# Starting every SBUF tile that TensorE reads at a multiple of 256 bytes, in a gated mix of sliding attention and a GEGLU FFN

## The chip, the cores and the metric

The kernel runs on one core of one Trainium2 chip. The metric is the device time in microseconds of one execution, as the median of several runs. Profiles are of one execution each, whose own time stands beside its span (from the first to the last instruction).

## The reference

For one sequence of 2,048 tokens with 512 channels in float32:

```python
g = sigmoid((x * gate_w).sum(-1))
qkv = x @ wqkv                       # 32 heads of 16 channels
# each query sees 8 keys: itself and 2, 4, ... 14 tokens back (those that exist)
a = softmax(q . k / 4, masked) . v @ wo
b = (gelu(x @ w_gate) * (x @ w_up)) @ w_down     # 1,792 hidden channels
out = g * a + (1 - g) * b
```

## The kernel before

**Split numbers.** Each float32 operand of a matmul is split into a rounded half `hi` and a rest `lo`, both of TensorE's faster float32 kind. A product is three matmuls: hi by hi, hi by lo, lo by hi. `split` (line 78) does that: ScalarE copies (line 82), VectorE subtracts (line 83).

**Halves of the tokens.** The work runs twice, for even tokens (`par` 0) and odd ones (`par` 1). Each half is a projection of x to keys and queries, values, and again keys and queries (`project`, three blocks `cb` 0, 1, 2), and then the FFN in 14 steps `f` of 128 hidden channels (`ffn`, `gate_up`, `down`). Between the two halves stand the second half's projections and the output projection of the first (`finish`, line 638).

**The matmuls.** `qkv_mm` (line 179) has 128 tokens of x as weights and 512 columns of `wqkv` as the moving operand; for `cb` 1, the values, two calls of 258 and 256 columns (line 205; the 257th column of the first is the gate's logit). `product` (line 411) has 128x128 of the gate and up weights as weights and 512 tokens of x, or of sums of x, as the moving operand; seven such products make an FFN step, by a scheme that saves the eighth. `down` (line 450) has hidden channels by tokens as weights and a row of `w_down` as the moving operand.

**The tiles.** Buffers come from one pool; `tl(tag)` (line 53) takes the next buffer of a tag, with the sizes of `COLS` and the counts of `BUFS` (lines 48 to 51). Tiles stand one behind the other in SBUF in the order in which their tags are first used. What TensorE reads:

- `A` (x, hi and lo), `S` (sums of x, also half of the weights of `cb` 0), `rt` (x of two chunks);
- `g0` and `g1`, two buffers each: gate and up weights of an FFN step, hi beside lo. Between FFN halves they hold split chunks of `wqkv` (`rooms`, line 137), each 2 x 258 = 516 columns wide;
- `d`: `w_down` of a step, and the weights of `cb` 2; `hh` and `hl`, six each: hidden channels, or attention's output; at `cb` 1 also the fourth chunk of the values' weights; `c`: split `wo` (and scratch).

**What sets the order.** In the first FFN half, weights come from HBM to `raw` (lines 349, 350, GpSimd's queue), VectorE combines quarters of them (360), ScalarE writes their negative as `lo` (380), a DMA on GpSimd's queue adds `raw` to it (381, an accumulate), ScalarE writes `hi` (383). The split tiles are stored to HBM (`keep`, line 392, SP's queue) and loaded back in the second half (line 376). Attention (lines 241 to 298) runs on VectorE in pieces that `pull` (327) hands out between the matmuls; keys, queries and values go through HBM (lines 194 and 196 on ScalarE's queue, 229 to 234 on SP's). A scheduler orders the recorded instructions of each engine, with attention at low priority.

Of the kernel before, what the change touches and what calls it, by code (L numbers as in the profile page):

```python
# [9 lines left out]
F32 = mybir.dt.float32  # L10
# [5 lines left out]
P = 128  # L16
S, D, F = 2048, 512, 1792
H, DH, W = 32, 16, 8
NT = S // P
NP = NT // 2  # L20
KC = D // P
FC = F // P
CU = 16 * DH
WQ = CU + 2
WT = KC * WQ
UC = 128
UH = UC // DH
NU = D // UC
WARM = 31
# [7 lines left out]
QW = 2 * P  # L37
# [3 lines left out]
def tile_gated_mix(ctx: ExitStack, tc: tile.TileContext, xt, wqkv, wff, wo, out):  # L41
    nc = tc.nc
    ctx.enter_context(nc.allow_non_contiguous_dma(reason="rows of 512 bytes"))
    pool = ctx.enter_context(tc.tile_pool(name="sb", bufs=1))
# [2 lines left out]

    BUFS = {"A": 6, "S": 8, "g0": 2, "g1": 2, "d": 4, "raw": 2, "hh": 6, "hl": 6, "c": 4, "s": 3,
            "r": 2, "rt": 4, "p": 4, "lg": 2}
    COLS = {"A": 1024, "S": 1024, "g0": 6 * WQ, "g1": 8 * WQ, "c": 2 * WQ, "d": 1024, "raw": 8 * QW,  # L50
            "hh": 2 * WQ, "hl": 2 * WQ}

    def tl(tag, dt=F32):
        return pool.tile([P, COLS.get(tag, 512)], dt, name=tag, bufs=BUFS[tag])

    def pair(tag):
        t = tl(tag, F32R)
        return t[:, :512], t[:, 512:1024]

    def bank(tag):  # L60
        return psum.tile([P, 512], F32, name=tag, bufs=BUFS.get(tag, 1))


    warm = pool.tile([P, P], mybir.dt.bfloat16, name="warm")
    nc.vector.memset(warm, 0.0)
    idle = bank("p")
    for _ in range(WARM):
        nc.tensor.matmul(idle[:, :P], warm, warm, start=True, stop=True)
    zero = pool.tile([W, UC], F32, name="zero")
    nc.vector.memset(zero, 0.0)  # L70
# [7 lines left out]
    def split(eng, hi, lo, raw, copy=None):  # L78
        if copy:
            copy(hi, raw)  # L80
        else:
            nc.scalar.activation(hi, raw, AF.Copy)
        eng.tensor_tensor(lo, raw, hi.bitcast(F32), op=OP.subtract)
# [3 lines left out]
    for par in range(2):  # L87
        for hh in range(2):
            for n, t in (("k", KS), ("v", VS)):
                t[par, hh] = dram.tile([2, W + S // 2, UC], F32, name=f"{n}s{par}{hh}")  # L90
                for c in range(2):
                    nc.gpsimd.dma_start(t[par, hh][c, :W], zero)
            QS[par, hh] = dram.tile([2, S // 2, UC], F32, name=f"qs{par}{hh}")
        for u in range(NU):
# [42 lines left out]
    def rooms():  # L137

        def of(*tags):
            for tag, n in tags:  # L140
                t = tl(tag, F32R)
                yield from (t[:, i * 2 * WQ:(i + 1) * 2 * WQ] for i in range(n))
        cols = of(("g1", 4))
        for _ in range(2):
            yield next(cols), next(cols)
        for _ in range(2):
            yield pair("S")
        cols = of(("g0", 3), ("g0", 3), ("hh", 1), ("hl", 1))
        for _ in range(KC):
            yield next(cols), next(cols)  # L150
        for _ in range(KC):
            yield pair("d")

    def load_cb(cb, kc, tag, room, dma=nc.sync):
        hi, lo = WC[cb, kc] = next(room)
        raw = tl(tag)
        n = 512
        if cb == 1:
            n = 2 * WQ
            for hh in range(2):  # L160
                dma.dma_start(raw[:, hh * WQ:(hh + 1) * WQ], wqkv[hh, 2, :, kc * WQ:(kc + 1) * WQ])
        else:
            dma.dma_start(raw[:, :n], wqkv[cb // 2, kc // 2, :, kc % 2 * 512:kc % 2 * 512 + 512])
        return lambda: split(nc.vector, hi[:, :n], lo[:, :n], raw[:, :n])
# [8 lines left out]
    def qkv_mm(ps, par, jj, cb, kcs, c0=0, cn=512):  # L173
        t = slice((jj % BT) * P, (jj % BT + 1) * P)
        for kc in kcs:
            xh, xl = X[par, jj // BT, kc]
            wh, wl = WC[cb, kc]
            for n, (a, w) in enumerate(((xh, wh), (xl, wh), (xh, wl))):
                nc.tensor.matmul(ps[:, :cn], a[:, t], w[:, c0:c0 + cn], start=(kc == 0 and n == 0),  # L179
                                 stop=(kc == KC - 1 and n == 2))  # L180
# [4 lines left out]
    def take(ps, par, jj, hh, vals, eng=None):  # L185
        st = tl(next(stages))
        n = CU if vals else 512
        if eng:
            eng.tensor_copy(st[:, :n], ps[:, :n])
        else:  # L190
            nc.scalar.activation(st[:, :n], ps[:, :n], AF.Copy)  # L191
        two = st.rearrange("p (a c d) -> p a c d", a=2, c=2)
        dst = VS[par, hh] if vals else KS[par, hh]
        nc.scalar.dma_start(rows(dst[:, W:], jj), two[:, 0])
        if not vals:
            nc.scalar.dma_start(rows(QS[par, hh], jj), two[:, 1])
        elif not hh:
            nc.scalar.activation(z[:, par, jj:jj + 1], ps[:, CU:CU + 1], AF.Copy)

    def project(par, cb, bg=iter(())):  # L200
        for jj in range(NP):
            if cb == 1:
                for hh in range(2):
                    ps = bank(next(names))
                    qkv_mm(ps, par, jj, 1, range(KC), hh * WQ, (WQ, CU)[hh])
                    take(ps, par, jj, hh, True)
            else:
                ps = bank(next(names))
                qkv_mm(ps, par, jj, cb, range(KC))
                take(ps, par, jj, cb // 2, False)  # L210
            next(bg, None)
            pull(2.7)
        done.add((par, cb))
        if cb == 1:
            en = pool.tile([P, NP], F32, name="en")
            nc.scalar.activation(en, z[:, par], AF.Exp, scale=-1.0)
            nc.vector.tensor_scalar_add(en, en, 1.0)
            nc.vector.reciprocal(g[:, par], en)
            nc.vector.tensor_scalar(gc[:, par], g[:, par], -1.0, 1.0, op0=OP.mult, op1=OP.add)
# [4 lines left out]
    def load_kq(par, u):  # L224
        hh, c = divmod(u, 2)
        k = pool.tile([P, 2 * NP - 1, UC], F32, name="k")
        q = pool.tile([P, NP, UC], F32, name="q")
# [99 lines left out]
    def pull(budget, key=None):  # L327
        credit[0] += budget
        while credit[0] > 0 and (key is None or key not in done):
            with tc.high_priority(offset=-BEHIND):  # L330
                c = next(fill, None)
            if c is None:
                credit[0] = 0.0
                return
            credit[0] -= c
        if key:
            credit[0] = 0.0
# [189 lines left out]
    def before():  # L527

        fetch_x(1, 1)
        yield  # L530
        room_x(1)
        for kc in range(KC):
            load_cb(0, kc, "r", room, nc.gpsimd)()
            yield
# [123 lines left out]


    room = rooms()  # L660
    room_x(0)
    for kc in range(KC):
        first = ((0, P), (P, 512 - P)) if not kc else ((0, 512),)
        sp = load_cb(0, kc, "c", room)
        if not kc:
            XR.update((i, tl("raw")) for i in range(2))
        for blk in range(2):
            for a, n in first if not blk else ((0, 512),):
                o = (2 * blk + kc // 2) * 512 + a
                nc.sync.dma_start(XR[kc % 2][:, o:o + n], xt[blk, :, kc, a:a + n])  # L670
            split_x(0, blk, kc, first if not blk else ((0, 512),), nc.vector.tensor_copy if not (kc or blk) else None)
            if not blk:
                sp()
    ps = [bank(next(names)) for _ in range(NP)]
# [6 lines left out]
    for kc in range(KC):  # L681
        load_cb(1, kc, "c", room)()
# [4 lines left out]
    for kc in range(KC):  # L687
        load_cb(2, kc, "c", room)()
    project(0, 1)
    combine(0)  # L690
    for _ in operands(0, 0):
        pass
    combine(1)
    project(0, 2)
    fetch_d(0)
    room = rooms()
    ffn(0)
    for kc in range(KC):
        load_cb(1, kc, "c", room)()
    project(1, 0, sums_x())  # L700
    fetch_o()
    for kc in range(KC):
# [53 lines left out]
```

## Time and profile before

| | us |
|---|---|
| median of 3 runs | 663.26 (662.86 to 665.01) |
| the profiled execution | 665.45 |
| its span | 663.6 |
| TensorE busy | 623.3 |
| VectorE busy | 518.5 |
| ScalarE busy | 338.8 |
| GpSimd busy | 136.1 |
| mean granted TensorE clock | 0.984 |

In profile lines PE is TensorE, PEld its weight loads, DVE VectorE, ACT ScalarE, POOL GpSimd, SP SyncE; a q behind a name is that engine's DMA queue. A line as `L411` is a line of the kernel. Busy time of TensorE counts overlapping matmuls by modelled ends, so "busy" is not "at its peak"; how far apart neighbouring matmuls start is the better measure of its pace.

### The profile page before, as it was taken

The numbers are of one execution on the slowest core, as the hardware profiler recorded it, in microseconds if no ns is written. First come the engines' busy times: TensorE is split into PE (matmuls) and PEld (weight loads), VectorE is DVE, ScalarE is ACT, GpSimd is POOL, SyncE is SP. The second block draws the span as 40 slices with busy tenths as digits, with TensorE's granted clock in tenths as the row PEclk, the third lists the DMA queues.
The fourth block names the chain that finished last, engine by engine and source line by source line (L and its number), as shares of the span: only waits on it lengthen the run. The fifth ranks groups of instructions, "written<-read, shape, count | busy, mean of one in ns | idle before, by whom it ended". The sixth has DMA issues, their size and how long they took to land.

```text
span 663.6 us, 8115 instructions
## 1 busy us (share of the span) xinstructions
PE 623.3 (94%) x2839; PEld 507.0 (76%) x2839; DVE 518.5 (78%) x567; ACT 338.8 (51%) x581; POOL 136.1 (21%) x161
## 2 busy tenths in 40 slices
PE   8999569998999998988999999799999999999997
PEld 7898447777778786776889888588878888878885
DVE  6939179988799789697984798988998999981241
ACT  5535057574667856558655422234445435444561
POOL 5012013132223222121110001342212222021100
PEclk9999979999999999998999999799999999999999
DMA  8688969999999999995669997954757472543113
GB/s 257 184 248 219 361 191 234 334 315 286 329 303 314 269 365 251 323 268 200 191 199 318 309 330 208 218 179 165 269 190 269 149 258 112 179 142 124 38 58 126
DMA packets 75336, 153.97 MB, mean 232 GB/s; under 512 B 7712, under 2 KB 43168, under 8 KB 71712
## 3 DMA queue, kind: packets, MB, share of 16 engines
q1 hardware_dynamic: 36000, 103.84, 43.9%
q0 software_dynamic: 13184, 37.04, 23.5%
q10 hardware_dynamic: 26112, 12.59, 6.5%
q8 instruction: 22, 0.36, 0.2%
q14 instruction: 18, 0.15, 0.1%
HBM read 80.76 MB, written 56.16 MB: 206 GB/s over the span
## 4 chain that ended last, share of the span: by engine, by line
PE 49%; DMA 26%; DVE 9%; issue 8%; ACT 5%; POOL 2%; ACTq 1%; SPq 0%; POOLq 0%; DVEq 0%
PE p L411 18%; DMA g<-raw 10%; PE p L179 7%; PE acc L179 7%; PE p L450 6%; PE acc L450 5%; PE p L638 3%; PE acc L638 3%; DMA raw<-wff 2%; DMA vs<-s 2%; DMA qs<-s 2%; DMA q<-qs 2%; DMA raw<-xt 2%; DVE prod L281 2%; DMA ws<-g 1%
## 5 line engine op out<-in xcount | busy, mean ns | idle before, releaser
L411 PE MATMUL p<-S,g 128*128 128x512 f32 x672 | 174.1, 400 | 18.9 <-ACT r L191 12.0
L411 PEld LDWEIGHTS p<-S,g 128*128 128x128 f32 x672 | 127.6, 191 | 51.6 <-ACT r L191 12.5
L411 PE MATMUL p<-A,g 128*128 128x512 f32 x504 | 133.4, 399 | 10.2 <-DMA g<-raw 6.2
L411 PEld LDWEIGHTS p<-A,g 128*128 128x128 f32 x504 | 95.0, 190 | 36.4 <-DMA g<-raw 9.4
L246 DVE TENSOR_TENSOR prod<-k,q 128x2048 f32<-128x2048 f32 x32 | 73.0, 2280 | 9.2 <-DMA q<-qs 9.0
L427 POOL TENSOR_TENSOR hl<-c,hh 128x512 fp32r<-128x512 f32 x28 | 45.4, 1622 | 160.4 <-ACT hh L426 117.1
L281 DVE TENSOR_TENSOR prod<-v,lg 128x2048 f32<-128x2048 f32 x32 | 75.0, 2343 | 0.8 <-DMA v<-vs 0.2
L450 PE MATMUL p<-d,hh 128*128 128x512 f32 x224 | 70.0, 401 | 4.9 <-ACT p L444 4.9
L248 DVE TENSOR_REDUCE lg<-prod 128x128 f32<-128x2048 f32 x32 | 73.0, 2281 | 0.3
L450 PE MATMUL acc<-d,hh 128*128 128x512 f32 x224 | 59.1, 395 | 0.0
L450 PEld LDWEIGHTS p<-d,hh 128*128 128x128 f32 x224 | 42.5, 191 | 16.3 <-ACT p L444 6.7
L426 ACT ACTIVATE hh<-c 128x512 fp32r<-128x512 f32 x56 | 35.2, 628 | 34.5 <-DVE c L424 34.1
L424 DVE TENSOR_TENSOR c<-c 128x512 f32<-128x512 f32 x56 | 38.4, 685 | 14.7 <-ACT c L523 14.1
L450 PEld LDWEIGHTS acc<-d,hh 128*128 128x128 f32 x224 | 42.0, 188 | 9.9 <-ACT hh L426 0.3
L463 ACT ACTIVATE rt<-p 128x512 f32<-128x512 f32 x48 | 28.0, 592 | 42.2 <-PE p L450 42.1
L420 DVE TENSOR_TENSOR c<-p,s 128x512 f32<-128x512 f32 x56 | 38.1, 682 | 13.5 <-PE p L411 13.1
L415 ACT ACTIVATE s<-p 128x512 f32<-128x512 f32 x56 | 32.8, 592 | 26.2 <-PE p L411 19.1
L450 PE MATMUL p<-d,hl 128*128 128x512 f32 x112 | 43.3, 401 | 0.0
L285 DVE TENSOR_TENSOR prod<-prod 128x1024 f32<-128x1024 f32 x32 | 39.5, 1235 | 0.3
L381 POOL DMA_DIRECT2D g<-raw x28 | 26.9, 1009 | 37.4 <-ACT g L380 32.3
L360 DVE TENSOR_TENSOR raw<-raw 128x256 f32<-128x256 f32 (+1 forms) x42 | 21.2, 507 | 16.9 <-DMA raw<-wff 11.6
L380 ACT ACTIVATE g<-raw 128x1024 fp32r<-128x1024 f32 (+1 forms) x28 | 26.6, 950 | 15.3 <-DVE raw L360 12.7
(150 smaller groups left out, 975.1 us busy)
## 6 DMA issues: line engine op xcount, KB each, us to landing
ws<-g SPq DMA_DIRECT2D x14, 1024.0 KB, 7.8
g<-ws SPq DMA_DIRECT2D x14, 1024.0 KB, 5.2
ws<-g SPq DMA_DIRECT2D x14, 768.0 KB, 8.6
g<-ws SPq DMA_DIRECT2D x14, 768.0 KB, 5.8
raw<-wff POOLq DMA_DIRECT2D x28, 256.0 KB, 8.1
g<-raw POOLq DMA_DIRECT2D x14, 512.0 KB, 10.8
ds<-d SPq DMA_DIRECT2D x14, 512.0 KB, 7.7
d<-ds SPq DMA_DIRECT2D x14, 512.0 KB, 6.0
```

The source lines that it names most:

```text
L179: nc.tensor.matmul(ps[:, :cn], a[:, t], w[:, c0:c0 + cn], start=(kc == 0 and n == 0), stop=(kc == KC - 1 and n == 2))
L246: nc.vector.tensor_tensor(prod, spans(k, jj), q[:, jj:jj + 2, None, :].to_broadcast([P, 2, W, UC]), op=OP.mult)
L248: nc.vector.tensor_reduce(lg[:, jj:jj + 2].rearrange("p j w h -> p (j w h)"), prod.rearrange("p j w (h d) -> p (j w h) d", d=DH), axis=AX. ...
L281: nc.vector.tensor_tensor(prod.rearrange("p j w (h d) -> p j w h d", d=DH), spans(v, jj).rearrange("p j w (h d) -> p j w h d", d=DH), lg[: ...
L285: nc.vector.tensor_tensor(prod[:, :, :4], prod[:, :, :4], prod[:, :, 4:], op=OP.add)
L411: nc.tensor.matmul(ps, w_, a_, start=(start and kc == 0 and n == 0), stop=(kc == 1 and n == 2), skip_group_check=True)
L420: nc.vector.tensor_tensor(c, ps, s, op=OP.add)
L424: nc.vector.tensor_tensor(ge, ge, up, op=OP.mult)
L426: nc.scalar.activation(hh_, ge, AF.Copy)
L427: eng.tensor_tensor(hl_, ge, hh_.bitcast(F32), op=OP.subtract)
L450: nc.tensor.matmul(pp, a[:, ts], w, start=(i == 0 and n == 0 and gr == 0), stop=(i == 1 and n == 2), skip_group_check=True)
L638: nc.tensor.matmul(pa, a, b, start=(not par and u == 0 and n == 0), stop=(u == NU - 1 and n == 2), skip_group_check=True)
```

## The change

No product, copy or DMA is added or taken out. The change gives tiles other sizes, so that those behind them begin elsewhere, and moves one chunk of weights to another tag.

- `g0` shrinks from 6 x 258 columns to 3 x 576 = 1,728, `g1` from 8 x 258 to 2,048, `c` goes from 516 to 576; `hh` and `hl` go from 516 to 512 columns. `warm` and `en` are padded.
- The values' chunk becomes 514 columns instead of 516: the 256 of the second head half first, then the 258 of the first. So both calls begin at a multiple of 256 columns.
- In `rooms` the values' eight pieces lie in two `g0` buffers and, now, one `g1` buffer, where the last two were in `hh` and `hl`; a piece is 576 columns wide instead of 516.

Start addresses modulo 256 bytes, from the two built programs (chunks inside a tile add 16 bytes each before, a multiple of 256 after):

| tiles | before | after |
|---|---|---|
| A, S, rt, d | 64 | 0 |
| g0, its two buffers | 64, 128 | 0, 0 |
| g1, its two buffers | 64, 128 | 0, 0 |
| c, four buffers | 192, 224, 0, 32 | 0 |
| hh, six buffers | 192, 224, 0, 32, 64, 96 | 0 |
| hl, six buffers | 128, 160, 192, 224, 0, 32 | 0 |

The scheduler makes another order from the changed program: 324 of 2,870 TensorE instructions, 127 of 567 of VectorE, 91 of 661 of ScalarE (its DMA issues counted), 20 of 250 on SP and 12 of 161 on GpSimd stand elsewhere.

```diff
+WA = 576
...
-    COLS = {"A": 1024, "S": 1024, "g0": 6 * WQ, "g1": 8 * WQ, "c": 2 * WQ, "d": 1024, "raw": 8 * QW,
-            "hh": 2 * WQ, "hl": 2 * WQ}
+    COLS = {"A": 1024, "S": 1024, "g0": 3 * WA, "g1": 8 * QW, "c": WA, "d": 1024, "raw": 8 * QW}
...
-    warm = pool.tile([P, P], mybir.dt.bfloat16, name="warm")
+    warm = pool.tile([P, P + 96], mybir.dt.bfloat16, name="warm")[:, :P]
...
-                yield from (t[:, i * 2 * WQ:(i + 1) * 2 * WQ] for i in range(n))
+                w = 512 if n == 4 else WA
+                yield from (t[:, i * w:(i + 1) * w] for i in range(n))
...
-        cols = of(("g0", 3), ("g0", 3), ("hh", 1), ("hl", 1))
+        cols = of(("g0", 3), ("g0", 3), ("g1", 3))
...
-            n = 2 * WQ
-            for hh in range(2):
-                dma.dma_start(raw[:, hh * WQ:(hh + 1) * WQ], wqkv[hh, 2, :, kc * WQ:(kc + 1) * WQ])
+            dma.dma_start(raw[:, :CU], wqkv[1, 2, :, kc * WQ:kc * WQ + CU])
+            dma.dma_start(raw[:, CU:CU + WQ], wqkv[0, 2, :, kc * WQ:(kc + 1) * WQ])
+            n = CU + WQ
...
-                    qkv_mm(ps, par, jj, 1, range(KC), hh * WQ, (WQ, CU)[hh])
+                    qkv_mm(ps, par, jj, 1, range(KC), (CU, 0)[hh], (WQ, CU)[hh])
...
-            en = pool.tile([P, NP], F32, name="en")
+            en = pool.tile([P, 64], F32, name="en")[:, :NP]
```

## The prediction

> **What bounds the kernel now.** I read the page's busy row first, then the table of stretches, the chain, and the waits of TensorE.
>
> ```profile
> PE 623.3 (94%) x2839; PEld 507.0 (76%) x2839; DVE 518.5 (78%) x567; ACT 338.8 (51%) x581; POOL 136.1 (21%) x161
> ```
>
> TensorE is 94% busy, but a busy TensorE can be slower than it need be. So I look at how far apart matmuls start. The chain of work that ended last merges matmuls that follow without a wait: start in us, length in us, line, count.
>
> ```profile
> 375.23 5.44 PE acc L179 x24
> ...
> 461.60 5.59 PE p L411 x24
> ...
> 643.98 5.56 PE p L638 x24
> ```
>
> All three are 24 matmuls of 128x128 by 128x512. The first takes 226.7 ns each, the others 232.9 and 231.7. The table of stretches (length, busy us and count by engine, clock, DMA share, GB/s) tells where TensorE is the limit:
>
> ```profile
> 60.00:80.00 20.00, 14.88 (x66) 12.01 (x64) 7.88 (x9) 3.72 (x9) 3.73 (x6) 0.99 1.02 310
> 80.00:110.00 30.00, 21.36 (x83) 16.39 (x84) 22.90 (x23) 17.18 (x27) 6.64 (x9) 0.83 0.78 231
> ...
> 140.00:180.00 40.00, 36.31 (x155) 28.56 (x154) 32.08 (x42) 23.86 (x40) 9.98 (x13) 1.00 1.04 306
> ...
> 500.00:540.00 40.00, 40.00 (x174) 32.30 (x173) 37.94 (x38) 18.96 (x31) 7.80 (x5) 1.00 0.57 205
> 540.00:580.00 40.00, 40.00 (x175) 32.52 (x174) 39.39 (x34) 19.70 (x32) 8.04 (x5) 1.00 0.51 180
> ```
>
> From 500 to 580 us TensorE never stops, and VectorE is nearly full beside it (39.39 of 40). From 110 to 300 us (first FFN half) TensorE loses some 4 us in most 40, with the DMA engines full (share 1.04). Around 75 to 87 us lies the one long stop:
>
> ```profile
> PE p L411 <- ACT r L191: 12.0, 1, 12.0
> PE p L411 <- DMA g<-raw: 6.2, 6, 1.7
> ```
>
> **Part 1: the starts of TensorE's tiles.** I call a tile's start address modulo 256 its residue. I took the start times of all 2,839 matmuls from the trace and joined them, in order, to the tile addresses of the built program. A matmul counts as equal when its moving operand, its own weights and the weights loaded beside it (those of the next matmul) have one residue. For 512 columns at full clock, without a stop (under 245 ns):
>
> ```
> unequal                             1480   232.5 ns
> equal                                861   228.9 ns
> of these, after 10 or more equal     273   226.7 ns
> unequal, after 12 without a stop    1296   232.5 ns
> ```
>
> So equal residues settle at 226.7 ns after about ten matmuls; unequal ones never do, however long they run. That it isn't the kind of work shows within one line: at line 411 with weights in the first g0 buffer (residue 64, as S) the mean is 228.9 ns (135 of them), in the second (residue 128) 233.4 ns (146). How busy ScalarE, VectorE, GpSimd or the DMA engines are at the time makes under 1 ns.
>
> After the change every such tile has residue 0, hence all are equal. No equal long run at residue 0 is in this trace, all of them are at 64; I take 0 to behave as 64 does. At most it saves 1480 x 5.8 ns = 8.6 us, plus 861 x 2.2 ns = 1.9 us: 10.5 us. By stretch, with each stretch's own counts and means: 0.65 before 110 us, 3.9 from 110 to 320 (first FFN half), 1.35 from 320 to 425 (projections and line 638), 4.1 from 425 to 637 (second FFN half), 0.5 at the end. Below, nothing is excluded: if the residue has to be 64, the saving is none.
>
> What of it reaches the end:
> - Before 110 us: inputs and the long stop set the pace. I count 0.3.
> - First FFN half: the g tiles come through a ring of DMAs (wff to raw, accumulate into g, 8.1 and 10.8 us to landing), which already ends several waits of TensorE. A faster TensorE will wait longer for it. Between 0 and 3.9 I take half, 1.95.
> - 320 to 425 us: hardly a stop; 1.2.
> - Second FFN half: 4.1, less what VectorE takes back. From 460 to 580 us VectorE is busy 39.55 + 37.94 + 39.39 = 116.9 of 120 us. TensorE would need only 117.6 there (2.4 us less), and VectorE must then run without a gap; its queue holds attention's products ahead of the adds that free TensorE's banks (line 420). I take 0.8 off: 3.3.
> - End: 0.5, nothing else is on the path.
>
> Sum: 0.3 + 1.95 + 1.2 + 3.3 + 0.5 = 7.25 us gained.
>
> A rule of the Trainium skill speaks against this: "TensorE: Matmul & The Clock Gate", in "Step-by-step: what each phase is for", says that the moving operand and the weights have SBUF read ports of their own, and that loading the next weights "doesn't steal SBUF read bandwidth from the running matmul". By it addresses change nothing and this part is 0; the rows above differ by 5.8 ns, so I follow the rows and keep the rule as a rival.
>
> **Part 2: narrow matmuls.** The 384 matmuls of the values' projection (called at line 205; 256 or 258 columns) stand about 120 ns apart, all unequal now. They become equal. Below: no gain. Above: the same 5.8 ns each, 2.2 us. Half as many columns take more than half of 226.7 ns already, and the weight load is busy beside them (18.29 of 20 us from 40 to 60 us), so I take 0.
>
> **Part 3: the values' chunks.** The split copies 514 columns instead of 516: 0.63 us for 516, so 2.4 ns less for each of 16 instructions, nothing. The loads stay at 16 DMAs of 128 or 129 KB (129 before). The padding of warm and en adds no instruction.
>
> **Part 4: the ring of g1.** The values' fourth chunk now takes a g1 buffer, not hh and hl. So the group-1 weights of f = 1 must wait for the end of the values' projection (near 62 us) where they had a buffer free earlier. By the program order their copy, their accumulate (512 KB) and their 1 MB store move back: the store from ahead of k and q on SP to behind them, and the 768 KB store of f = 1's group 0 ahead of k and q. That group's accumulate has landed by 70.1 us (GpSimd's wait), while k and q went out at 73.3, so SP isn't held. What changes is what the DMA engines carry in the long stop, which ends when ScalarE's 128 KB stores of q free tile r:
>
> ```profile
> g<-raw POOLq DMA_DIRECT2D x14, 512.0 KB, 10.8
> qs<-s ACTq DMA_DIRECT2D x19, 128.0 KB, 3.2
> ```
>
> Added: 512 KB, 1.7 us at the 310 GB/s of that stretch, 3.4 if reading and writing both count. Taken out of its early part: a 1 MB store, 3.4 us. From -3.4 to +3.4 I take +0.8, half of the nearest row. The next reload of raw moves some 8 us back, to about 78 us; its data is needed past 110. Later uses of g1 stand one buffer on with the same parity between FFN steps. The load of the second half's first g1 (at 346.6 us now) goes behind its g0 at 375 us; FFN starts only near 412 us, so this costs nothing, and if that cover went, 5.2 us.
>
> **Part 5: order.** The scheduler sets 324 of 2,870 TensorE instructions elsewhere (by 39 places at most), 127 of 567 on VectorE, 20 of 250 on SP. The waits it could remake are the named ones of the first FFN half, 0.3 to 1.7 us each, some 10 us in all. I take 0, within -3 and +3.
>
> **Sum.** -7.25 + 0.8 = -6.45 us. The profiled execution took 665.45 us (span 663.6 and 1.85 around it), 2.2 above the median of 663.26. It would become 659.0; the median 656.8.
>
> **Rivals.**
> 1. *Everything arrives, 652.8 us.* The DMA ring has slack, VectorE closes its gaps: 663.26 - 10.5. For it: the waits for g are short (1.7 us at most). Against: the DMA share of 1.04 and VectorE at 98%. 15%.
> 2. *No difference from addresses, 664.1 us.* The port rule holds, or residue 0 differs from 64; only part 4 is left, 663.26 + 0.8. Against: the split within line 411. With it goes that the gain is real and VectorE and the ring take most of it back (662). Together 17%.
> 3. *Slower, 666.8 us.* The added accumulate lands in the full DMA stretch at 62 to 87 us and takes its whole 10.8 us from ScalarE's stores, so the stop grows from 12.0 to 22.8 us; 10.8 - 7.25 leaves +3.55. It decides once the stop grows by more than 9.3 us (7.25 and the 2 us that can be told). For it: the clock already fell there (0.83 from 80 to 110 us). Against: 1 MB leaves the same stretch. With bad luck in the order: 13%.
>
> The forecast itself, 653 to 661 us, has 55%.
>
> **Chances and range.** No change means within 0.3%, 2.0 us, about what a measurement can tell: 661.3 to 665.3. Faster: the forecast, rival 1 and a little of rival 2, 0.72. Same 0.15, slower 0.13. The range takes rival 1 with some of the negative end of part 4, and rival 2's number: 651 to 664.2.
>
> **What would show it.** Right: runs of 24 in the chain take 5.44 us at lines 411, 450 and 638 as well; mean ns of one at line 411 falls from 400 towards 390; TensorE's count in 500 to 540 us rises from 174 towards 176. Wrong: the spacing of line 638 stays at 231 ns (residue 0 is no cure), or the named waits for g and for line 420 grow by more than 4 us, or the stop before 87 us passes 20 us.

## The result, and the profile after

The changed kernel takes 654.53 us (651.48 to 657.37, six runs) where the kernel before took 664.23 in the same comparison; the ratio is 0.9853 [0.982, 0.9886]. In two later comparisons it took 650.73 (0.9808 [0.9756, 0.986]) and 652.98 (0.9806 [0.9762, 0.985]); the brackets are 95% intervals. Over all 18 runs the mean is 652.8 us, with a standard error of 0.75; that of the kernel before over all comparisons is 664.3. The gain is some 11.5 us, 1.7%. Here and below, ratios and means leave out three runs of a slower state: one each of the kernel before, the kernel with two families and the one with products on GpSimd. The forecast was 656.8, with 651 to 664.2 as its range.

The profiled execution took 651.48 us (span 649.7, granted clock 0.983). It is the fastest of its six runs, 3 us under their median, so I compare its stretches and rates with those of before, and times by the medians and means. Line numbers are one or two higher than before: 413, 452 and 640 are what 411, 450 and 638 were.

The busy row of the changed kernel's page, and then runs of 24 matmuls from its chain (start, length, line, count):

```profile
PE 616.9 (95%) x2839; PEld 507.8 (78%) x2839; DVE 519.5 (80%) x567; ACT 338.3 (52%) x581; POOL 137.6 (21%) x161
```

```profile
346.96 2.89 PE p L181 x24
...
630.52 5.44 PE p L640 x24
637.54 5.44 PE p L640 x24
```

The same instructions, 6.4 us less of TensorE's busy time, and VectorE as before. At line 640, 24 matmuls now take 5.44 us, or 226.7 ns each; they took 5.56. The narrow ones at line 181 have not moved: 2.89 us for 24, or 120 ns.

The table of stretches, with the same columns as before:

```profile
60.00:80.00 20.00, 15.90 (x69) 12.89 (x68) 8.65 (x12) 3.84 (x8) 3.55 (x5) 0.95 1.04 322
80.00:110.00 30.00, 26.81 (x104) 20.26 (x102) 29.75 (x26) 20.35 (x33) 8.29 (x11) 0.92 0.92 266
140.00:180.00 40.00, 36.67 (x154) 29.54 (x154) 33.37 (x43) 25.47 (x43) 12.17 (x16) 0.96 0.97 301
500.00:540.00 40.00, 38.51 (x169) 31.20 (x168) 39.52 (x33) 15.19 (x27) 8.97 (x5) 1.00 0.52 177
540.00:580.00 40.00, 39.74 (x174) 32.14 (x173) 39.28 (x39) 21.50 (x34) 9.70 (x6) 1.00 0.50 169
```

From 60 to 110 us TensorE now starts 173 matmuls (69 and 104) instead of 149. From 140 to 180 it starts no more than before (154 and 155), and from 500 to 540 fewer, 169 against 174, with VectorE at 39.52 of 40. So the profile puts the largest piece of the gain where I did not look for it, before 110 us, and little into these stretches of the two FFN halves, where most of the faster matmuls are. The waits of TensorE (total, times, longest) say the same:

```profile
PE p L413 <- DMA g<-raw: 7.0, 4, 3.0
PE p L413 <- DVE c L422: 6.8, 5, 3.3
PE p L413 <- ACT r L193: 4.1, 1, 4.1
```

The long stop, 12.0 us on ScalarE's tile r, is 4.1.

I then joined start times and tile addresses as in the prediction. All 2,322 matmuls of 512 columns that follow without a stop start 227.1 ns apart; before it was 231.2 over 2,341. From the same starts, three things for each FFN half: its length, the *pace excess* (what its matmuls take above 226.7 ns, or 120 for narrow ones), and its stops without a matmul. Pace and stops leave out every matmul that touches time at half the clock, of which a half has 0 to 20 us, and so they leave out the long stop as well; the lengths leave out nothing. The profiles are single ones. Microseconds; the other kernels are those of the experiments:

```
                          first half             second half
                          length pace  stops     length pace  stops
before                     248.0  4.3   21.5      223.4  4.2    3.2
after                      236.9  0.6   13.9      220.6  0.3    8.8
after, profiled again      238.7  0.5   12.2      219.1  0.3    9.3
after, a third time        239.2  0.6   15.8      220.5  0.4   10.7
all at residue 64          240.4  0.5   13.2      222.1  0.4   10.3
no pair equal              238.6  4.6   13.9      222.9  5.1    8.4
addresses, order of before 247.9  2.7   20.4      219.9  2.7    2.9
order, mixed addresses     239.0  4.5   17.7      221.7  4.6    7.6
```

The pace excess is gone in the changed kernel (0.6 and 0.3). But the first half is 236 to 241 us long in all profiles with the new order and 248 in both with the old one, whatever its pace; and in the second half the stops are longer in every kernel with the new order.

The second half of before has 6.8 us at half clock, those of the changed kernel 3.4, 0 and 0. Half of such time is lost; with it taken off the lengths (an estimate), the halves compare so:

```
                          first half     second half
before                     241.2          220.0
after, three profiles      228.4 to 230.7 218.9 to 220.5
all at residue 64          231.9          220.4
no pair equal              230.1          222.9
addresses, order of before 239.4          218.2
order, mixed addresses     233.9          221.7
```

### The profile page after: what moved, and what is told of

The parts are those of the page before. It is cut to its first block, busy times and chain, and to the rows that moved or that the text cites. A ratio compares the mean times of both kernels' runs of the same rounds, so it can differ in the third digit from the quotient of the medians.

```text
span 649.7 us, 8121 instructions
## 1 busy us (share of the span) xinstructions
PE 616.9 (95%) x2839; PEld 507.8 (78%) x2839; DVE 519.5 (80%) x567; ACT 338.3 (52%) x581; POOL 137.6 (21%) x161
## 4 chain that ended last, share of the span: by engine, by line
PE 35%; DVE 21%; DMA 20%; issue 17%; ACT 4%; POOL 1%; SPq 1%; ACTq 0%; DVEq 0%; POOLq 0%
PE p L413 16%; DMA g<-raw 7%; PE p L452 5%; DVE prod L283 4%; PE acc L452 4%; PE acc L181 3%; PE p L181 3%; DMA c<-wqkv 2%; DVE c L422 2%; DMA ws<-g 2%; DMA v<-vs 2%; DVE prod L287 2%; DVE prod L248 2%; PE acc L640 2%; PE p L640 2%
## 5 line engine op out<-in xcount | busy, mean ns | idle before, releaser
L413 PE MATMUL p<-S,g 128*128 128x512 f32 x672 | 172.2, 398 | 6.6 <-ACT r L193 4.1
L413 PEld LDWEIGHTS p<-A,g 128*128 128x128 f32 x504 | 95.8, 193 | 41.7 <-DVE c L422 10.5
L429 POOL TENSOR_TENSOR hl<-c,hh 128x512 fp32r<-128x512 f32 x28 | 46.6, 1663 | 159.3 <-ACT hh L428 107.7
L452 PE MATMUL p<-d,hh 128*128 128x512 f32 x224 | 68.3, 393 | 3.0 <-ACT p L446 3.0
L452 PE MATMUL acc<-d,hh 128*128 128x512 f32 x224 | 56.3, 390 | 0.1
L426 DVE TENSOR_TENSOR c<-c 128x512 f32<-128x512 f32 x56 | 40.1, 716 | 15.3 <-ACT c L525 14.2
L452 PE MATMUL acc<-d,hl 128*128 128x512 f32 x112 | 32.7, 389 | 0.0
L525 ACT ACTIVATE c<-p 128x512 f32<-128x512 f32 x28 | 16.7, 597 | 29.5 <-PE p L413 27.7
```

The costliest lines, as they stand in the source:

```text
L413: nc.tensor.matmul(ps, w_, a_, start=(start and kc == 0 and n == 0), stop=(kc == 1 and n == 2), skip_group_check=True)
L426: nc.vector.tensor_tensor(ge, ge, up, op=OP.mult)
L429: eng.tensor_tensor(hl_, ge, hh_.bitcast(F32), op=OP.subtract)
L452: nc.tensor.matmul(pp, a[:, ts], w, start=(i == 0 and n == 0 and gr == 0), stop=(i == 1 and n == 2), skip_group_check=True)
```

## Experiments

Two theories at the outset. **Pace**: equal residues are the gain, and the order is worth nothing, as the prediction has it. **Order**: the moved chunk makes another order of DMAs, and that is the gain. For the pace itself, a rule of *pairs* (a matmul is fast if it and the weights loaded beside it are equal) stood against *runs* (it needs a row of equal ones).

**The same order, other addresses.** Three kernels with exactly the changed kernel's order of instructions (pads apart), and that kernel itself. All tiles at residue 64:

```diff
-    warm = pool.tile([P, P + 96], mybir.dt.bfloat16, name="warm")[:, :P]
+    warm = pool.tile([P, P + 128], mybir.dt.bfloat16, name="warm")[:, :P]
```

The other two put 64-byte pads between families of tiles (`pad` makes one and clears it): one pad behind `g0`, or four that leave no pair of operands equal.

```diff
+    def pad(n):
+        nc.gpsimd.memset(pool.tile([P, 16], F32, name=f"pad{n}"), 0.0)
```

> The changed kernel once more, on the chip of the next three, so that they can be compared with it. All tiles of TensorE at residue 0. Both theories: about 9.7 us (1.5%) under the kernel before, 512-column matmuls 227 ns apart. Its long stop before the first FFN half was 4.1 us in one profile (12.0 before); if that is the new order's doing it is again near 4.

> The changed kernel with every tile 64 bytes further on: all at residue 64, none at a multiple of 256, instructions and their order as after. Theory 1 (what counts is that moving operand and weights have the same residue): the same time as after within 1.5 us, 512-column matmuls 227 ns apart. Theory 2 (tiles must begin at multiples of 256): 232.5 ns apart for some 2,340 of them, 2,340 x 5.8 ns = 13 us over after, near the time before.

> The changed kernel with four pads of 64 bytes between tags: A, hh, hl at residue 0, g1 and c at 64, rt and S at 128, g0 and d at 192, so that no matmul has equal residues; instructions and their order as after (four small memsets on GpSimd at the start more). Theory 1 (addresses alone make the gain): all 512-column matmuls 232.5 ns apart, 13 us over after, and 3.3 us over the kernel before, which has 861 equal ones. Rival (the new ring of g1 and the new order make part of the gain, such as the 8 us by which the long stop was shorter): under the kernel before, by up to 5 us, with a long stop near 4 us.

> The changed kernel with one pad of 64 bytes behind g0: d, hh, hl (the operands of the down matmuls) at residue 64, all others at 0; order as after. Down matmuls are equal among themselves, those of gate and up too, 576 of 2,423 pairs are unequal (blocks that follow each other, the projection with d, the output projection). If each matmul's pace depends on its own tiles and the weights loaded beside it: 576 x 5.8 ns = 3.3 us over after. If the fast pace needs some ten equal ones in a row first, as the trace of before showed: the blocks of 3 to 12 of the FFN are too short for it, and by the means of that trace for each place in a row it comes to 7 us over after.

Measured, as median, ratio to before, and mean with its standard error:

```
the changed kernel         650.73   0.9808 [0.9756, 0.9860]   651.2 +- 1.5
all at residue 64          657.80   0.9901 [0.9869, 0.9933]   657.5 +- 0.7
one pad, two families      658.31   0.9904 [0.9869, 0.9939]   657.4 +- 0.8
no pair equal              660.05   0.9932 [0.9904, 0.9961]   659.9 +- 0.6
```

Two findings. With no pair equal, the kernel is still 4.4 us faster than before: the order does that, not the addresses. And residue 64 has the full pace, as the chain of its profile shows, but not the full gain:

```profile
634.00 5.44 PE p L640 x24
641.03 5.44 PE p L640 x24
```

In the kernel with no pair equal the same runs take 5.49 us and its matmuls start 232.0 ns apart on average. With two families, 1,764 matmuls whose pair is equal, in short blocks between unequal ones, take 229.3 ns and not 226.7: runs, not pairs. By its time (657.4) it can't be told from the copy at 64 (657.5), so the pace that it lacks did not reach the end there.

**The pace by itself.** A kernel of 22 streams of 48 matmuls each, with nothing else going on, in which the byte positions of the moving operand and the weights are chosen. It ran once, at a clock of 0.999. In the table fp32r is TensorE's faster float32 kind and bf16 a 16-bit one; positions count from the starts of tiles that themselves lie at residue 128:

```python
for kind, n, at in STREAMS:
    for k in range(COUNT):
        mo, so = (v // size for v in at(k))
        nc.tensor.matmul(ps[k % 4][:, :n], s[:, so:so + P], m[:, mo:mo + n], start=True, stop=True)
```

> Not the reference's work: x is copied to the output, and TensorE runs 22 streams of 48 matmuls each, all else idle. A stream has one difference between the start of the weights and the start of the moving operand, in bytes: 0, 4, 16, 32, 64, 96, 128, 192, 240, 256 for 512 columns, then both moved by 64 and by 128, the moving operand moved by 64 alone, then alternating residues 0 and 64 with the moving operand equal to its own weights, and with it equal to the weights loaded beside it, then 256 columns at 0, 64, 128, and bfloat16 at 0, 64, 128. Theory 1 (equal residues modulo 256): 226.7 ns at 0 and 256 and where both are moved, 232 to 233 at every other difference. Rival A (modulo 64 or 128): 226.7 at 64 or 128 too. Rival B (the pace of before came from the work around it, not from addresses): all alike. If the clash is between reading the moving operand and loading the next weights beside it, the last alternating stream is fast and the one with its own weights slow; if between a matmul's own two operands, the other way round. 256 columns: 120 ns at every difference if the weight load sets their pace.

Mean spacing of matmuls 13 to 47 of each stream, in ns, by how many bytes modulo 256 the weights stand ahead of the moving operand:

```
fp32r, 512 columns   4: 232.4   16: 233.3   32: 233.4   64: 233.4   96: 234.3
                     128: 232.4   192: 228.8   240: 228.3   256: 226.7
  both at 64: 226.7   both at 128: 226.7   both at 0, last: 226.7   moving +64: 228.9
  equal to its own weights only: 231.9      to the next weights only: 231.8
fp32r, 256 columns   0: 120.0   64: 117.8   128: 118.7
bf16, 512 columns    0: 215.8   64: 215.9   128: 215.9
```

The first stream, with both at 0 too, began with matmuls some 427 ns apart and is not in the table. The equal streams need about four to ten matmuls to settle: with both at 64 they begin 229, 229, 233, 236, 224, 231, 236, 228, 233, 231, and then 226, 227 without end. The residue itself is no matter, only the difference; both pairs must be equal. It is lopsided: weights 192 or 240 bytes ahead, which is 64 or 16 behind, cost 2 ns, while 4 to 128 ahead cost 6 to 8. The weight loads differ too; behind the first bar stand busy us and the mean ns of one:

```profile
L64 PEld LDWEIGHTS p<-mr,sr 128*128 128x128 f32 x912 | 163.6, 191 | 49.8 <-ACT sr L56 16.3
...
L64 PEld LDWEIGHTS <-sb 128*128 128x128 bf16 x144 | 14.0, 98 | 16.8
```

A bf16 load takes 98 ns of the 215.8 between two matmuls, an fp32r load 191 of 226.7. So there is less room beside an fp32r matmul. Whether reads of the two operands are in each other's way is not shown: no run here separates the cause.

**The order apart from the addresses.** First most of the addresses without the order: the kernel before, its values' chunks still in `hh` and `hl`, with `g0`, `g1` and `c` sized so that most tiles begin at residue 64 (1,568 equal pairs, 889 before); its order is exactly that of before. Then the order without the addresses: one line of the change, which gives exactly the changed kernel's order on every engine and leaves mixed residues (675 equal pairs; `d` and the tiles behind it begin elsewhere than before).

```diff
-        cols = of(("g0", 3), ("g0", 3), ("hh", 1), ("hl", 1))
+        cols = of(("g0", 3), ("g0", 3), ("g1", 3))
```

> The kernel before, with its own ring and its own order of instructions, in which g0, g1, c and the chunks in g0 have sizes that are multiples of 256 bytes: all of A, S, rt, g0, g1, c, d at residue 64, hh and hl at various ones as before (one small memset more). 1,568 of 2,423 pairs are equal (889 before). Theory 1 (addresses alone): 679 x 5.8 ns = 3.9 us under the kernel before if each pair counts by itself, 3.6 us by the means for each place in a row. Rival (the gain of the change needs its new order): no difference from before, with a long stop of 12 us.

> The kernel before with one line of the change: the values' fourth chunk in a g1 buffer, not hh and hl. Sizes as before, so residues stay mixed (675 of 2,423 pairs equal, 889 before). Every engine's order is then that of the changed kernel. Theory (order and ring shorten the first FFN half by some 8 to 10 us, whatever the pace of the matmuls): 4 to 7 us under the kernel before, like the all-unequal run, with the long stop near 4 us and the first FFN half near 238 us (248 before). Rival (the gain is the addresses'): 1 us over the kernel before.

```
addresses, order of before   661.45   0.9972 [0.9941, 1.0002]   662.2 +- 0.7
order, mixed addresses       658.51   0.9912 [0.9881, 0.9944]   659.0 +- 0.8
```

The one line gives 5.3 us (664.3 to 659.0), about half of the gain; the addresses under the old order give about 2, and that interval touches no difference. The waits of TensorE at the long stop, first with the addresses only, then with the line only:

```profile
PE p L412 <- ACT r L192: 10.7, 1, 10.7
```

```profile
PE p L411 <- ACT r L191: 5.3, 1, 5.3
```

**What of the order shortens the stop.** The trace of SyncE's queue, before and then after (start, length, what is issued, count):

```profile
62.40 2.81 SPq L392 DMA_DIRECT2D ws<-g  x2
65.43 1.04 SPq L233 DMA_DIRECT2D v<-vs  x1
...
73.33 0.32 SPq L233 DMA_DIRECT2D k<-ks  x1
```

```profile
62.66 1.47 SPq L394 DMA_DIRECT2D ws<-g  x1
67.18 0.32 SPq L235 DMA_DIRECT2D k<-ks  x1
...
78.60 14.13 SPq L394 DMA_DIRECT2D ws<-g  x2
```

Before, the first of the two stores at 62.40 is the 1 MB of step 1's `g1`; after, it is among those at 78.60, behind `k` and `q`, and the 768 KB store of step 1's `g0`, which was at 78.45, has gone ahead of them (62.66). The loads of `k` go out 6 us earlier. So I held the 1 MB store back in the kernel before: its accumulate stays early, the addresses stay mixed, and a 64-byte DMA on SyncE's queue into the store's target, recorded with the last keys, makes it wait. With that, the scheduler sends the 768 KB store ahead of `k` here too. In the built programs little else stands elsewhere than before up to the end of the long stop: two neighbours on ScalarE (0.6 us each), and three of VectorE's subtractions of line 360, which come earlier here. After it much does: in all 271 TensorE instructions and 98 of VectorE, nearly as many as in the changed kernel, though in another order than there.

```diff
+        if (par, hh, vals, jj) == (0, 1, False, 3):
+            WS[1, 1] = dram.tile([P, 8 * QW], F32, name="ws11")
+            nc.sync.dma_start(WS[1, 1][:1, :16], st[:1, :16])
...
-            WS[f, i] = dram.tile(list(w.shape), F32, name=f"ws{f}{i}")
+            if (f, i) not in WS:
+                WS[f, i] = dram.tile(list(w.shape), F32, name=f"ws{f}{i}")
```

> The kernel before with its own ring and sizes, in which the 1 MB store of group 1 of step 1 has to wait for a 64-byte DMA that takes its bytes from a copy of the first projection's third block, so that it stands behind k and q on SP, as in the changed kernel, and not ahead of them. Theory (that store, sent into the stretch where ScalarE's stores of k and q must land, makes the long stop): stop near 4 us, 4 to 8 us under the kernel before. Rival (other parts of the order, such as the accumulate that moved, shorten it): stop near 12 us, no difference.

It takes 658.72 us, 0.9918 [0.9887, 0.995], mean 659.1 +- 0.8: as much as the line gains. The long stop is 5.0 us:

```profile
PE p L415 <- ACT r L191: 5.0, 1, 5.0
```

The row of 74 to 88 us, before and in this kernel, shows it best:

```profile
74.00:88.00 14.00, 1.97 (x7) 1.28 (x7) 1.56 (x3) 1.89 (x4) 0.00 (x0) 0.70 0.93 350
```

```profile
74.00:88.00 14.00, 7.85 (x25) 5.66 (x25) 7.38 (x10) 4.22 (x8) 0.54 (x1) 0.76 1.04 375
```

TensorE starts 25 matmuls there instead of 7. The 1 MB goes out after the stretch in which ScalarE's stores of keys and queries, on which the tile r hangs, share the DMA engines (share 0.93 to 1.04 in these rows). The shorter stop is thus put down to the places of the two stores. That the 5 us in time are theirs alone is likely, since two kernels with different orders behind the stop gain the same, but it is not shown.

**Residue 0 against 64.** One difference was left: the changed kernel and its copy at 64 have the same order and the same pace, and stood 6 us apart. Both were run again, with a kernel in which TensorE's tiles are at 0 as in the changed kernel, and tiles that it doesn't read lie elsewhere (`raw`, `k`, `q`, `lg`, `prod` at 64, `v`, `tb`, `o` at 96), by pads of 64, 192 and 160 bytes.

> The changed kernel again, beside its copy at residue 64. In the first call it was 7 us under that copy (650.7 against 657.8) with the same pace of matmuls and the same order. If residue 0 helps something else than TensorE (the DMA engines), the same 5 to 7 us again; if it was chance, within 3 us of it.

> The changed kernel with every tile 64 bytes on, again. Chance: within 3 us of the changed kernel beside it. Residue 0 helps the DMA engines too: 5 to 7 us over it.

> The changed kernel, all tiles of TensorE at residue 0 as there, but those that it doesn't read moved off: raw, k, q and the products at 64, v and attention's output at 96, as in the kernel before. Order as after. If the 4 us between the changed kernel (652.8 over 18 runs) and its copy at residue 64 (656.9 over 15) come from these tiles (DMA engines and VectorE reading them at residue 0): 657. If they come from TensorE's tiles standing at 0, or were chance: 653.

```
the changed kernel              652.98   0.9806 [0.9762, 0.9850]   652.8 +- 1.3
all at residue 64               656.68   0.9864 [0.9821, 0.9908]   656.0 +- 1.3
only TensorE's tiles at 0       656.02   0.9886 [0.9866, 0.9907]   656.0 +- 0.7
```

Pooled, the copy at 64 takes 656.9 +- 0.7 (15 runs) and the changed kernel 652.8 +- 0.75 (18): 4.1 +- 1.0 us apart. The third sides with the copy, though its TensorE reads from residue 0. That points to tiles that TensorE doesn't read; which of them, and why, stays open. Half clock isn't it: one less the granted clock, times the span, is 10.0 us in the mean of the one and 10.1 of the other.

One candidate is the packets of 512 bytes on SyncE's queue, nearly all of attention's stores (`os` from `tb`): they take 29.0 to 29.2 ns on average in the four profiles with the changed kernel's layout, and 30.5 to 33.7 in the nine others. "DMA: Bandwidth & Descriptors" in the Trainium skill, in "How a descriptor splits into AXI transactions", has it that a start off a multiple of 256 bytes costs extra beats. But the median is 27 ns in all of them and packets of 4,096 bytes take 159 ns in both kinds, so this page's account is neither borne out nor shown to be worth 4 us.

**A stop beside VectorE.** In the second half of the changed kernel TensorE waits for the adds of line 422. Theory: GpSimd has time to spare there (46.6 of 220 us), so it could take the products on `ge` from VectorE and make the kernel faster.

```diff
-        nc.vector.tensor_tensor(ge, ge, up, op=OP.mult)
+        (eng if key[1] else nc.vector).tensor_tensor(ge, ge, up, op=OP.mult)
```

> The changed kernel, in which the second product of gelu and up (the one that is put off to the next step) runs on GpSimd in the second FFN half, where VectorE does it now: 14 x 0.7 us less on VectorE, 14 x some 1.7 us more on GpSimd (22% busy there). Theory (VectorE, full from 460 to 580 us, takes back the gain of the second FFN half; it stops for 9 to 11 us there): stops 3 to 6 us less, 2 to 5 us under the changed kernel. Rival (the later hidden tile holds up the down matmuls instead): as long or longer, with more waits at line 452.

It takes 658.29 us (0.9898 [0.9866, 0.993], mean 657.3 +- 1.1), slower than the changed kernel. TensorE's wait for those adds from 420 to 640 us, first in the changed kernel, then here:

```profile
PE p L413 <- DVE c L422: 3.5, 4, 1.5
```

```profile
PE p L413 <- DVE c L422: 7.5, 4, 2.7
```

The theory fell: relieved of 14 instructions, VectorE lets TensorE wait longer (the unchanged wait is 3.4 to 3.5 us in four other profiles of this order). The order isn't the changed kernel's either: 138 TensorE instructions stand elsewhere. What orders VectorE's queue there stays open.

## Why the prediction was right, and where its steps were not

The total was right: 656.8 forecast, medians of 650.7 to 654.5 and a mean of 652.8 measured, inside the range. Its make-up was not. The forecast had 7.25 us from the pace and a loss of 0.8 from the ring. The runs, one step after the other, from means: the order 5.3 +- 0.9 (before to the one line), the pace 2.1 +- 1.1 (from there to all at residue 64; 3.0 +- 0.9 from the kernel with no pair equal), and 4.1 +- 1.0 from residue 64 to 0. The kernels of these steps differ in residues of tiles that TensorE doesn't read as well, so the last, unexplained effect may be in the first two. Two errors of opposite sign, and a gain I had no term for, came out near the right sum: that was luck. That the mean is the number of rival 1, 652.8, is luck too, for most of the pace did not arrive.

- **The spacing: right.** It was to fall to 226.7 ns at lines 411, 450 and 638; line 640 shows 5.44 us for 24, and the mean of all is 227.1, since short runs don't settle. That residue 0 behaves as 64 was right of the pace (226.7 in the streams for both 0 and 192, and 5.44 us for 24 at 0 and 64), and wrong of the kernel (4.1 us).
- **The rule of the two read ports: not for this kind.** The Trainium skill's "TensorE: Matmul & The Clock Gate" has, in "Step-by-step: what each phase is for", that weight loads take no read bandwidth from the running matmul, by which addresses would make no difference. In the streams they make none for bf16 (215.8 and 215.9 ns), and do for fp32r of 512 columns (226.7 against 228 to 234); that the ports are the cause is not shown. So the half of rival 2 that rests on it fell; its other half, that most of the pace is taken back, is near what happened (2 to 3 us of 10.5 arrived), and what the order gave came on top. That VectorE and the ring take it back is shown only in part (the two FFN halves below).
- **First FFN half, 1.95 of 3.9: 0 to 2.** Half was a guess between ends. The pace excess fell by 3.7 us, yet 247.9 us with better addresses stands beside 248.0 without, and 239.0 with mixed addresses beside 236.9 to 240.4 with equal ones. With half clock taken off, 1.8 us are left between the first two, and the new order has 230.1 and 233.9 without the full pace against 228.4 to 231.9 with it. The DMA engines are full here (share 0.96 to 1.05 from 110 to 300 us after the change), which fits a ring of DMAs that sets the length, but no run tests it.
- **Second FFN half, 3.3 of 4.1: the pace brings 1 to 4, and the new order takes about as much.** The pace excess fell by 3.9 us and the half by 2.8 to 4.3 in the three profiles, but with half clock taken off it is 220.0 before and 218.9 to 220.5 after. Under the old order the better addresses bring 1.8 (218.2); the new order without the pace is 1.7 to 2.9 longer (221.7, 222.9). Stops grew from 6.8 us (the 3.2 and one of 3.6 that runs into half clock) to 9.3 to 10.7, and the wait for VectorE's adds from 1.2 to 3.5. I had seen that VectorE must then run without a gap, and priced that at 0.8. TensorE's count from 500 to 540 us fell to 169, where I expected a rise to 176.
- **Narrow matmuls, 0: right.** 120.2 ns after, 119.8 before (32 of the 384 were equal already, not none). In the streams equality even costs 2 ns at 256 columns (120.0 against 117.8).
- **Values' chunks, 0:** no run tested it by itself.
- **The ring of g1, +0.8: the wrong sign, and past the bound of -3.4.** The working had both pieces: 512 KB added, 1 MB taken out of the early part, the stop ending when ScalarE's stores free r. I priced the 1 MB by its bytes over the bandwidth, 3.4 us, and took the added accumulate as nearest. With that store held back the kernel is 5.2 us faster (659.1 against 664.3), and the stop fell from 12.0 to 5.0. The step that failed is to cost a transfer in a full DMA stretch by its share of the bytes; what counted was which transfers stood ahead of those that are waited for (1 MB gone from there, 768 KB come). Part of the line's 5.3 goes along with the clock: with it, time lost to half clock (worked out as above) falls from a mean of 12.1 to 7.7 us, with the store moved only to 11.0, so the clock isn't the whole of either. The copy at 64 is back at 10.1, so at equal clock the pace would be nearer 4 us and the line nearer 3 (an estimate, with the 0.6 us per us of the last section).
- **Order, 0 within 3:** the first FFN half is some 9 us shorter where the new order is (239.0 with the one line, 248.0 before), 7 of it the long stop. No run takes the remainder apart.
- **Rival 3, the stop grows to 22.8: fell.** It shrank, with the accumulate added (3.1 to 5.6 us in all profiles of the new order).
- **Mean ns of one at line 411 falling to 390: a bad sign to name.** It is 398 and 401, as before. That figure counts modelled ends that stops and half clock lengthen. The distance of starts is the measure.

Open: what makes residue 0 of other tiles worth 4 us, what takes the pace back in the first half, and what orders VectorE's queue in the second.

## What to carry to other kernels

Price a moved DMA by what it stands ahead of when the engines are full, not by its bytes: sending a 1 MB store 16 us later, with a 768 KB one ahead in its place, cut a stop by 7 us, and the kernel was 5 us faster, where all the faster matmuls gave 2 to 4. A faster bottleneck engine is worth only what the others leave: where DMA share or VectorE was near 1, little of the pace arrived here. Before two profiles' stretches are compared, take off the time at half clock, which moves from run to run. To credit a layout change, hold the instruction order fixed and move only the addresses; a change of tile sizes nearly always changes both.

## What the runs showed of the hardware

- In fp32r matmuls of 512 columns the spacing depends on the starts of moving operand and weights modulo 256: 226.7 ns when equal for four to ten in a row, 232 to 234 when the weights are 4 to 128 bytes ahead, 228 to 229 when 192 or 240 ahead. bf16 (215.8) doesn't have it, and 256 columns (117.8 to 120.0) hardly.
- The spread between runs of one kernel goes in part with the granted clock. Over 72 runs of the kernel before, each us lost to half clock goes with 0.6 us more time (correlation 0.6). In one comparison the changed kernel's runs go from 647.15 us at clock 0.992 to 655.71 at 0.978.
